# The first block's beginning rearranged in a two-branch kernel (state-space convolution plus a Mish feed-forward)

## The chip, the cores and the metric

The kernel runs on one core of one Trainium2 chip. The metric is the device time of one execution in microseconds. Its engines are PE (matrix products), DVE (VectorE), ACT (ScalarE), POOL (GpSimd) and SP (which here only issues transfers). ACT and POOL issue transfers too.

## What is computed

The input u has 2048 rows of 640 values. Each row is normalized; the result xn goes through two branches, whose sum is added to u.

```
xn  = (u - mean) / sqrt(var + 1e-5)                      # per row of 640
A   = causal convolution of xn over the rows, one kernel per column,
      K = 2 * Re(sum_n C_n * exp(A_n * dt * l)), plus xn * D_skip
h   = xn @ w1 + b1                                       # w1: 640 x 1728
B   = (h * tanh(softplus(h))) @ w2                       # w2: 1728 x 640
out = u + A + B
```

## The kernel before

**Tiles.** The 2048 rows are worked off in four blocks (or chunks) of TB = 512 columns of the transposed x, so that the 640 columns of x lie in KD = 5 groups ("channels") of 128 partitions. The 1728 hidden values lie in NF = 14 tiles f, of 128 or (f = 8) 64. A block multiplies w1's tile f with x (15 products of 512 columns; names h and tr in the trace), sends the result through a chain of activation steps on ACT and DVE, and multiplies it with w2 into five accumulators (acc). Single precision is reached by splitting each operand into a high and a low half-precision part: `hi_...` rounds on ACT, `lo_...` takes the rest on DVE, and each product is made three times: hh, lh (weight low), hl (x low). In blocks 1 to 3, pairs of tiles f go through a scheme with fewer products (the five parts `one` to `four` of `mm1_pair`), for which sums of weights and of x are prepared.

**Side work.** Beside this stand: the weight roundings in block 0; the statistics and normalization of the next chunk's x; the convolution, which for these inputs becomes two running sums per channel and chunk ("skip" steps: `skip_a` on ACT L709 to L711, the scans `skip_b` and `skip_c` on DVE at L715 and L719, `skip_e` at L729, `skip_d` on ACT); the 29 checks of the weights' size (`load_chk`, `chk` on ACT at L675 and L678) whose result decides at the end whether a general version must run; POOL's accumulating transfers that join the parts.

**Order.** The order of every engine is fixed when the kernel is built. For the beginning (block 0's products f = 0, 1, 2 and all before them) it is written out by hand, in the part that the change replaces. From there the class `Plan` sets it: each step has an engine, an assumed cost, the steps that it needs, buffers that it takes and drops, and a due time; whenever an engine is free in the plan's own clock, the ready step with the earliest need is put next. PE's order is given, and other steps get due times from it. `pl.end["m1", 0, f]` and the clocks in `Plan({...})` say when the handwritten part is assumed to end on each engine. `edge` and `t0, t1` give due times to the skip steps and the checks, as positions in PE's order (`start(b, f)` is the begin of block b's tile f).

**The beginning.** X0 holds block 0's four row tiles of 128 x 640. `stats0(i)` takes the statistics of tile i on DVE (L597 to L599, L1260) and the power -0.5 on POOL (L1261). `norm0(i)` normalizes on DVE (L1201). `norm0_a(i)`, which is defined but not called, does it on ACT. `to_t0(i)` transposes tile i on PE, five channels, into the accumulators' banks (L1217). `hi0(k, c)` and `lo0(k, c)` round channel k of one half: CA is columns 0 to 255 (tiles 0 and 1), CB columns 256 to 511 (tiles 2 and 3). `mm1_part(f, kinds, c, ks)` makes products (L755). `load_w1`, `hi_w1` (L522), `lo_w1` (L526) bring and split the weights. `fill(n)` keeps PE busy with products of the identity matrix. The queues of SP and ACT share the loads: column halves of tiles 0 and 1, then the row halves (64 partitions on each queue) of w1(0), tile 2, w1(1) and tile 3.

Of the kernel before, what the change touches and what calls it, by code (L numbers as in the profile page):

```python
# [422 lines left out]
def body(ctx: ExitStack, tc: tile.TileContext, x, xT, logA, Aim, Cr, Ci, logdt, vec, w1, w1T, w2, w2T, out):  # L423
# [65 lines left out]
    NCHK = NF + 3 * KD  # L489
    pl = Plan({"PE": 20.8, "ACT": 16.1, "DVE": 17.9, "SP": 15.0, "POOL": 15.0})  # L490
    tiles = lambda pool, name, n, shape: [pool.tile(shape, F32, name=f"{name}{j}") for j in range(n)]
# [421 lines left out]
    def whole():  # L913
# [53 lines left out]
        for f in range(3):  # L967
            pl.end["m1", 0, f] = (16.95, 18.55, 20.75)[f]

# [167 lines left out]
        for k in range(KD):  # L1137
            add(("x0s", k), V, 0.62, x0_sum, k, rel=start(0, 9))
        edge = [start(1, 4), start(2, 0), start(2, 11), start(3, 5), start(3, 11)]
        todo = [(c, k) for c in range(NB) for k in range(KD)]  # L1140
# [20 lines left out]

        t0, t1 = start(1, 4), start(3, 11)
        for j in range(NCHK):
# [33 lines left out]
    mv0 = tmp.tile([P, NT, 2], F32, name="mv0")  # L1197
    rs0 = tmp.tile([P, 2, NT], F32, name="rs0")

    def norm0(i):  # L1200
        v.tensor_scalar(X0[:, i], X0[:, i], mv0[:, i, 0:1], rs0[:, 0, i:i + 1], op0=OP.subtract, op1=OP.mult)  # L1201

    def norm0_a(i):
        v.scalar_tensor_tensor(rs0[:, 1, i:i + 1], mv0[:, i:i + 1, 0], -1.0, rs0[:, 0, i:i + 1], op0=OP.mult, op1=OP.mult)
        a.activation(X0[:, i], X0[:, i], AF.Identity, bias=rs0[:, 1, i:i + 1], scale=rs0[:, 0, i:i + 1])

# [18 lines left out]
    def load_x0(i):  # L1225
        for e, c in ((sp, slice(0, P // 2)), (a, slice(P // 2, P))):
            e.dma_start(X0[c, i], xr[0, i, c])

    def fill(n):
        for _ in range(n):  # L1230
            pe.matmul(TR[:, 0:P], ident, ident, start=True, stop=True)

    with tc.manual_schedule():

        for i in range(2):
            sp.dma_start(X0[:, i, 0:320], xr[0, i, :, 0:320])  # L1236
            a.dma_start(X0[:, i, 320:D], xr[0, i, :, 320:D])
        for f in range(6):
            pl.take("w", ("w1", f))
            if f < 2:  # L1240
                pl.take("w", ("w2", f))
        load_w1(0, (sp, a))
        load_x0(2)
        load_w1(1, (sp, a))
        load_x0(3)
        a.activation(warm, one, AF.Sigmoid)
        load_w1(2)
        sp.dma_start(cv[:, 0:24], vec)
        load_w1(3)
        load_w2(0)  # L1250
        load_w1(4)
        load_w2(1)
        load_w1(5)
        S = [list(stat_ops(mv0, X0[:, i], i)) for i in range(NT)]

        def stats0(i):
            for o in S[i]:
                o()
            r = rs0[:, 0, i:i + 1]
            v.tensor_scalar(r, mv0[:, i:i + 1, 1], EPS, None, op0=OP.add)  # L1260
            g.tensor_tensor(r, r, half, op=OP.pow)  # L1261

        fill(11)
        stats0(0)
        stats0(1)
        norm0(0)
        to_t0(0)
        hi_w1(0)
        norm0(1)
        to_t0(1)  # L1270
        for k in KS:
            hi0(k, CA)
        lo_w1(0)
        stats0(2)
        mm1_part(0, ("hh", "lh"), CA, start=True, ks=KS)
        hi_w1(1)
        lo0(KS[0], CA)
        lo0(KS[1], CA)
        mm1_part(1, ("hh",), CA, start=True)
        for f in range(2):  # L1280
            mm1_part(f, ("hl",), CA, ks=KS[:2])
        hi_w1(2)
        stats0(3)
        norm0(2)
        mm1_part(2, ("hh",), CA, start=True)
        to_t0(2)
        lo0(KS[2], CA)
        norm0(3)
        lo0(KS[3], CA)
        lo0(KS[4], CA)  # L1290
        mm1_part(2, ("hl",), CA, ks=KS[:2])
        for f in range(3):
            mm1_part(f, ("hl",), CA, ks=[KS[2]])
        to_t0(3)
        for k in KS[3:]:
            for f in range(3):
                mm1_part(f, ("hl",), CA, stop=f == 0 and k == KS[4], ks=[k])
        for k in KS:
            hi0(k, CB)
        lo_w1(1)  # L1300
        hi_w1(3)
        mm1_part(0, ("hh", "lh"), CB, start=True, ks=KS)
        for k in KS:
            lo0(k, CB)
        mm1_part(1, ("hh",), CB)
        mm1_part(0, ("hl",), CB, stop=True, ks=KS)
        lo_w1(2)
        lo_w1(3)
        for f in (1, 2):
            if f > 1:  # L1310
                mm1_part(f, ("hh",), CB)
            mm1_part(f, ("hl",), CB)
            mm1_part(f, ("lh",), slice(0, TB), stop=True)
# [39 lines left out]
```

## Time and profile before

| what | us |
|---|---|
| median of 3 runs | 359.85 (359.8 to 360.6) |
| the profiled execution | 359.29 |
| its span, first to last instruction | 357.5 |
| PE busy | 350.6 |
| DVE busy | 311.1 |
| ACT busy | 296.3 |
| POOL busy | 50.4 |

A row of the timeline gives the start and the length of one instruction or of several merged ones, its engine, line and operands, and in brackets how long the engine had been idle and what ended that. "PEld" is a weight load, which overlaps the products. "SPq" and "ACTq" are issues of transfers. Lengths of pipelined products overlap, so their distance, not their length, tells the cost. A row of the busy time in stretches gives the stretch, its length, each engine's busy time with its count of instructions, the granted clock of PE, the share of DMA time and GB/s. Line numbers are those of the kernel before.

### The profile page before, as it was taken

Reading aid. Unit: us, or ns where it says so; the run is one execution under the profiler, and the core shown is the slowest. Engines: PE = TensorE matmul, PEld = TensorE weight load, DVE = VectorE, ACT = ScalarE, POOL = GpSimd, SP = SyncE. Lnnn points to the kernel's source line nnn. Section 1 sums busy time; section 2 is a strip of 40 time slices with the busy share of each in tenths; the row PEclk is TensorE's granted clock in tenths of the full one; section 3 lists DMA queues with packets and bytes.
Section 4 is the critical chain, followed back from the end, with each engine's and each line's share of the span. In section 5 each row is a group of like instructions: output and inputs, shape, how many; then the busy total and the mean of one; then the engine's idle time right before and its main releaser. Section 6 shows DMA issues by size and latency. Waiting matters only on the chain.

```text
span 357.5 us, 6018 instructions
## 1 busy us (share of the span) xinstructions
PE 350.6 (98%) x2167; PEld 211.5 (59%) x2167; DVE 311.1 (87%) x585; ACT 296.3 (83%) x614; POOL 50.4 (14%) x72
## 2 busy tenths in 40 slices
PE   7999999999999999999999999999999999999995
PEld 6754444444666665665566666566566666566543
DVE  5989989989998999999999986899997888775552
ACT  3599999978488799889989897989978989868740
POOL 2100020000013041000103343000003552000000
PEclk9999999999999999999999999999999999999999
DMA  7879975105109954911256973941111994201003
GB/s 238 279 240 296 337 247 174 73 1 183 39 21 194 335 165 127 296 24 39 64 179 128 202 181 91 278 170 35 33 35 20 166 232 89 55 0 31 0 16 141
DMA packets 26036, 48.75 MB, mean 136 GB/s; under 512 B 3576, under 2 KB 6928, under 8 KB 26000
## 3 DMA queue, kind: packets, MB, share of 16 engines
q1 hardware_dynamic: 19152, 34.21, 29.8%
q0 software_dynamic: 6240, 13.11, 17.8%
q10 hardware_dynamic: 608, 0.98, 0.8%
q8 instruction: 19, 0.31, 0.4%
q14 instruction: 17, 0.14, 0.2%
HBM read 39.10 MB, written 5.26 MB: 124 GB/s over the span
## 4 chain that ended last, share of the span: by engine, by line
PE 95%; DMA 1%; DVE 1%; SPq 0%; ACT 0%; issue 0%; DVEq 0%
PE acc L825 48%; PE h L793 18%; PE h L773 14%; PE tr L793 12%; DMA x<-in_A_u_dram 1%; PE h L755 1%; PE tr L755 1%; PE acc L1217 0%; PE acc L839 0%; PE acc L836 0%; PE acc L837 0%; DVE w1l L526 0%; DVE st L598 0%; SPq L1236 0%; DVE st L597 0%
## 5 line engine op out<-in xcount | busy, mean ns | idle before, releaser
L825 PE MATMUL acc<-hi,w2h 128*128 128x512 f16 x273 | 100.9, 379 | 0.0
L825 PE MATMUL acc<-hi,w2l 128*128 128x512 f16 (+1 forms) x265 | 99.7, 379 | 0.0
L825 PE MATMUL acc<-lo,w2h 128*128 128x512 f16 x253 | 93.3, 379 | 0.0
L825 PEld LDWEIGHTS <-w2h 128*128 128x128 f16 x526 | 51.2, 98 | 48.4 <-issue 1.3
L863 ACT ACTIVATE s<-h,cv 128x512 f32<-128x512 f32 (+1 forms) x51 | 30.9, 605 | 23.6 <-PE h L793 18.4
L793 PEld LDWEIGHTS <-w1h 128*128 128x128 f16 x432 | 42.3, 98 | 10.7
L887 DVE SCALAR_TENSOR_TENSOR A<-p,A 128x512 f32<-128x512 f32 (+1 forms) x56 | 38.2, 682 | 7.2 <-ACT p L882 7.0
L825 PEld LDWEIGHTS <-w2l 128*128 128x128 f16 x273 | 25.6, 98 | 30.7 <-issue 1.1
L872 ACT ACTIVATE p<-s,kc 128x512 f32<-128x512 f32 (+1 forms) x56 | 40.1, 715 | 0.5
L882 ACT ACTIVATE p<-p,kc 128x512 f32<-128x512 f32 (+1 forms) x56 | 40.0, 714 | 0.2
L877 ACT ACTIVATE p<-p,kc 128x512 f32<-128x512 f32 (+1 forms) x56 | 39.9, 713 | 0.2
L905 DVE SCALAR_TENSOR_TENSOR lo<-A,hi 128x512 f16<-128x512 f32 x52 | 35.3, 680 | 3.6 <-ACT hi L894 3.3
L867 DVE SCALAR_TENSOR_TENSOR A<-h,bs,s 128x512 f32<-128x512 f32 (+1 forms) x51 | 33.0, 647 | 6.2 <-ACT s L863 6.0
L894 ACT ACTIVATE hi<-A 128x512 f16<-128x512 f32 (+1 forms) x56 | 34.9, 624 | 3.6 <-DVE A L887 3.4
L518 POOL DMA_DIRECT2D r<-in_xT_dram x15 | 13.7, 1094 | 126.8 <-ACT r L736 60.3
L773 PEld LDWEIGHTS <-w1h 128*128 128x128 f16 (+1 forms) x174 | 15.3, 99 | 20.3 <-issue 3.3
L715 DVE TENSOR_TENSOR_SCAN g<-g,car,kc 128x512 f32<-128x512 f32 x20 | 25.6, 1278 | 1.1 <-ACT g L709 1.1
L793 PEld LDWEIGHTS <-w1l 128*128 128x128 f16 x216 | 21.1, 98 | 8.4 <-issue 0.3
L719 DVE TENSOR_TENSOR_SCAN g<-g,car,g 128x512 f32<-128x512 f32 x20 | 25.5, 1276 | 0.1
L793 PE MATMUL tr<-xh,w1h 128*128 128x256 f16 x90 | 24.5, 273 | 0.1
L793 PE MATMUL tr<-xl,w1h 128*128 128x256 f16 x90 | 24.5, 273 | 0.0
L793 PE MATMUL tr<-xh,w1l 128*128 128x256 f16 x90 | 24.5, 273 | 0.0
(174 smaller groups left out, 728.7 us busy)
## 6 DMA issues: line engine op xcount, KB each, us to landing
w<-in_w_dram SPq DMA_DIRECT2D x23, 320.0 KB, 4.7
w<-in_w2T_dram SPq DMA_DIRECT2D x15, 288.0 KB, 6.4
w<-in_B_w_dram SPq DMA_DIRECT2D x13, 320.0 KB, 3.5
w<-in_w1T_dram SPq DMA_DIRECT2D x13, 320.0 KB, 6.6
x<-in_A_u_dram SPq DMA_DIRECT2D x12, 320.0 KB, 5.0
xt<-in_xT_dram SPq DMA_DIRECT2D x15, 256.0 KB, 5.5
r<-in_xT_dram POOLq DMA_DIRECT2D x15, 256.0 KB, 6.0
xt<-r POOLq DMA_DIRECT2D x15, 256.0 KB, 4.1
```

Of the source, the lines that this page charges most:

```text
L715: v.tensor_tensor_scan(g1[:, 1:], g1[:, 1:], zero.to_broadcast([P, TB]), car[:, 1, k:k + 1], op0=OP.add, op1=OP.add)
L773: pe.matmul(o, w, x, start=(j == 0), stop=(j == len(order) - 1))
L793: pe.matmul(o, p, q, start=start and n == 1, stop=n == 3 * len(w), skip_group_check=True)
L825: pe.matmul(o, w, x, start=start, stop=stop)
L863: a.activation(pl["s", b, f][:n, c], src(b, f) if h is None else h, AF.Sigmoid, bias=cv[:n, f:f + 1], scale=1 / SH)
L867: v.scalar_tensor_tensor(pl["A", b, f][:n, c], src(b, f) if h is None else h, bs[:n, f:f + 1], pl["s", b, f][:n, c], op0=OP.add, op1=OP.mult)
L872: a.activation(pl["p", b, f][:n], pl["s", b, f][:n], AF.Arctan, bias=one[:n], scale=-1.0)
L877: a.activation(p, p, AF.Square, bias=pi4[:n], scale=2.0)
L882: a.activation(p, p, AF.Tanh, bias=mb[:n], scale=MG)
L887: v.scalar_tensor_tensor(A, pl["p", b, f][:n], MC, A, op0=OP.add, op1=OP.mult)
L894: a.activation(hi[:n], A, AF.Copy, scale=MA * SA / SH)
L905: v.scalar_tensor_tensor(lo, A, MA * SA / SH, hi[:n], op0=OP.mult, op1=OP.subtract)
```

## The change

The two column halves of tile 0 are each split in two row halves, one on each queue; tile 1 keeps its column halves. Weights and tiles 2 and 3 come whole on SP's queue, in the order w1(0), w1(1), tile 2, tile 3. The warm-up activation (with the table load) follows directly on ACT's three issues. Tiles 0, 2 and 3 are normalized on ACT, whose `norm0_a` no longer uses DVE; tile 1 stays on DVE. `hi_w1(0)`, `hi_w1(1)` and `lo_w1(0)` stand ahead of the rounding of x, and for each channel the products hh and lh of f = 0 and hh of f = 1 follow its rounding. The low weight parts are spread between the low parts of x, and their products of half CA come earlier. The plan's clocks, the due times of the skip steps of chunks 1 to 3 and the beginning of the weight checks are changed.

```diff
-    pl = Plan({"PE": 20.8, "ACT": 16.1, "DVE": 17.9, "SP": 15.0, "POOL": 15.0})
+    pl = Plan({"PE": 19.95, "ACT": 15.3, "DVE": 16.8, "SP": 15.0, "POOL": 15.0})
...
-            pl.end["m1", 0, f] = (16.95, 18.55, 20.75)[f]
+            pl.end["m1", 0, f] = (17.0, 18.1, 19.9)[f]
...
-        edge = [start(1, 4), start(2, 0), start(2, 11), start(3, 5), start(3, 11)]
+        edge = [start(1, 4), start(2, 0), start(3, 2), start(3, 6), start(3, 13)]
...
-        t0, t1 = start(1, 4), start(3, 11)
+        t0, t1 = start(1, 0), start(3, 11)
...
+    nm0 = tmp.tile([P, 2, NT], F32, name="nm0")
...
     def norm0_a(i):
-        v.scalar_tensor_tensor(rs0[:, 1, i:i + 1], mv0[:, i:i + 1, 0], -1.0, rs0[:, 0, i:i + 1], op0=OP.mult, op1=OP.mult)
-        a.activation(X0[:, i], X0[:, i], AF.Identity, bias=rs0[:, 1, i:i + 1], scale=rs0[:, 0, i:i + 1])
+        a.activation(nm0[:, 0, i:i + 1], mv0[:, i:i + 1, 0], AF.Copy, scale=-1.0)
+        a.activation(nm0[:, 1, i:i + 1], nm0[:, 0, i:i + 1], AF.Identity, scale=rs0[:, 0, i:i + 1])
+        a.activation(X0[:, i], X0[:, i], AF.Identity, bias=nm0[:, 1, i:i + 1], scale=rs0[:, 0, i:i + 1])
...
     def load_x0(i):
-        for e, c in ((sp, slice(0, P // 2)), (a, slice(P // 2, P))):
-            e.dma_start(X0[c, i], xr[0, i, c])
+        sp.dma_start(X0[:, i], xr[0, i])
...
-        for i in range(2):
-            sp.dma_start(X0[:, i, 0:320], xr[0, i, :, 0:320])
-            a.dma_start(X0[:, i, 320:D], xr[0, i, :, 320:D])
+        for c in (slice(0, 320), slice(320, D)):
+            for e, p in ((sp, slice(0, P // 2)), (a, slice(P // 2, P))):
+                e.dma_start(X0[p, 0, c], xr[0, 0, p, c])
+        sp.dma_start(X0[:, 1, 0:320], xr[0, 1, :, 0:320])
+        a.dma_start(X0[:, 1, 320:D], xr[0, 1, :, 320:D])
...
-        load_w1(0, (sp, a))
+        a.activation(warm, one, AF.Sigmoid)
+        load_w1(0)
+        load_w1(1)
         load_x0(2)
-        load_w1(1, (sp, a))
         load_x0(3)
-        a.activation(warm, one, AF.Sigmoid)
...
-        def stats0(i):
-            for o in S[i]:
+        def stats0(i, done=0):
+            for o in S[i][done:]:
...
-        fill(11)
+        fill(10)
         stats0(0)
         stats0(1)
-        norm0(0)
+        norm0_a(0)
         to_t0(0)
-        hi_w1(0)
         norm0(1)
         to_t0(1)
+        hi_w1(0)
+        hi_w1(1)
+        lo_w1(0)
         for k in KS:
             hi0(k, CA)
-        lo_w1(0)
+            mm1_part(0, ("hh", "lh"), CA, start=k == KS[0], ks=[k])
+            mm1_part(1, ("hh",), CA, start=k == KS[0], ks=[k])
+        hi_w1(2)
+        mm1_part(2, ("hh",), CA, start=True)
         stats0(2)
-        mm1_part(0, ("hh", "lh"), CA, start=True, ks=KS)
-        hi_w1(1)
+        for o in S[3][:2]:
+            o()
         lo0(KS[0], CA)
...
+        stats0(3, 2)
+        norm0_a(2)
+        norm0_a(3)
+        hi_w1(3)
+        for k, w in zip(KS, (None, None, 1, 2, 3)):
+            if k != KS[0]:
+                lo0(k, CA)
             for f in range(3):
                 mm1_part(f, ("hl",), CA, stop=f == 0 and k == KS[4], ks=[k])
+            if k == KS[1]:
+                to_t0(2)
+            if w:
+                lo_w1(w)
+                if w < 3:
+                    mm1_part(w, ("lh",), CA)
+                if w == 1:
+                    to_t0(3)
         for k in KS:
             hi0(k, CB)
...
+            mm1_part(0, ("hh", "lh"), CB, start=k == KS[0], ks=[k])
+            mm1_part(1, ("hh",), CB, ks=[k])
         for k in KS:
             lo0(k, CB)
...
+        mm1_part(0, ("hl",), CB, stop=True)
+        mm1_part(1, ("lh", "hl"), CB, stop=True)
+        mm1_part(2, ("hh", "lh", "hl"), CB, stop=True)
         a.activation(bs, cv[:, 0:NF], AF.Copy, scale=SH)
...
-        pl.drop(("w1", f), 17.0)
+        pl.drop(("w1", f), 15.0)
```

More of the change, by code (lines that the diff above doesn't have):

```diff
@@ L1274, in body @@
+        mm1_part(2, ("hh",), CA, start=True)
         stats0(2)
-        mm1_part(0, ("hh", "lh"), CA, start=True, ks=KS)
-        hi_w1(1)
+        for o in S[3][:2]:
+            o()
         lo0(KS[0], CA)
[L1278 to L1295, printed above, removed]
+        stats0(3, 2)
[5 more added lines that the diff above has]
+                lo0(k, CA)
             for f in range(3):
                 mm1_part(f, ("hl",), CA, stop=f == 0 and k == KS[4], ks=[k])
+            if k == KS[1]:
[6 more added lines that the diff above has]
+                    to_t0(3)
@@ L1298, in body @@
         for k in KS:
             hi0(k, CB)
-        lo_w1(1)
-        hi_w1(3)
-        mm1_part(0, ("hh", "lh"), CB, start=True, ks=KS)
+            mm1_part(0, ("hh", "lh"), CB, start=k == KS[0], ks=[k])
+            mm1_part(1, ("hh",), CB, ks=[k])
         for k in KS:
             lo0(k, CB)
[L1305 to L1313, printed above, removed]
+        mm1_part(0, ("hl",), CB, stop=True)
```

## The prediction

> **What bounds the kernel now.** I read the page's busy times first, then the chain of waits, then the busy time in stretches, and last the timeline of the first 20 us, where the change acts.
>
> ```profile
> PE 350.6 (98%) x2167; PEld 211.5 (59%) x2167; DVE 311.1 (87%) x585; ACT 296.3 (83%) x614; POOL 50.4 (14%) x72
> ...
> 20.75 3.24 PE h L773 x15
> ...
> 96.23 1.97 PE h L793 x18
> ...
> 353.05 0.12 PE h L847
> ```
>
> ```profile
> 90.00:96.20 6.20, 6.20 (x42) 3.84 (x40) 5.99 (x16) 2.68 (x7) 0.00 (x0) 1.00 0.20 56
> 96.20:108.60 12.40, 12.40 (x87) 8.24 (x85) 12.08 (x44) 9.46 (x19) 2.61 (x3) 1.00 0.18 53
> ...
> 114.10:174.20 60.10, 60.04 (x391) 37.18 (x389) 58.77 (x103) 55.51 (x121) 9.10 (x13) 1.00 0.54 158
> 174.20:241.30 67.10, 67.10 (x450) 43.39 (x448) 61.27 (x101) 59.62 (x134) 14.79 (x19) 1.00 0.63 168
> 241.30:271.20 29.90, 29.90 (x195) 18.50 (x193) 28.66 (x47) 27.49 (x62) 0.00 (x0) 1.00 0.11 31
> 271.20:295.90 24.70, 24.70 (x170) 16.40 (x169) 20.66 (x31) 22.03 (x51) 12.85 (x16) 1.00 0.80 159
> 295.90:336.90 41.00, 41.00 (x277) 26.04 (x275) 28.68 (x55) 32.75 (x70) 3.28 (x5) 1.00 0.18 34
> ```
>
> PE is busy 98%, and in the stretches (length, then PE, weight loads, DVE, ACT, POOL, clock, DMA share, GB/s) its busy time equals the length, but for 0.06 us in the third row. So from 20.75, where the planned part begins with the products of f = 3, to 353.17, PE simply works off 332.4 us. Two things follow. The re-spread side work has nothing to win (0.06 us); it can only lose. And what the beginning wins is handed through to the end: every microsecond by which the products of f = 0..2 are done earlier than 20.75 is a microsecond of the span, as long as the planned part stays full.
>
> **The beginning, before.**
>
> ```profile
> 0.72 0.87 SPq L1236 DMA_DIRECT2D x<-in_A_u_dram  x2
> ...
> 3.70 0.49 DVE L597 BATCH_NORM_STATS2 st<-x 128x6 f32<-128x320 f32 x1 [2.73 <-DMA x<-in_A_u_dram]
> ...
> 4.94 0.48 DVE L597 BATCH_NORM_STATS2 st<-x 128x6 f32<-128x320 f32 x1
> 5.11 0.57 POOL L1261 TENSOR_TENSOR rs<-rs,kc 128x1 f32<-128x1 f32 x1 [3.61 <-DVE rs L1260]
> 5.21 1.28 ACT L1246 ACT_TABLE_LOAD   x1 [5.21 <-DMA x<-in_A_u_dram]
> ...
> 6.09 0.15 DVE L1260 TENSOR_SCALAR rs<-mv 128x1 f32<-128x1 f32 x1
> 6.16 0.60 DVE L1201 TENSOR_SCALAR x<-x,mv,rs 128x640 f32<-128x640 f32 x1
> 6.33 0.86 POOL L1261 TENSOR_TENSOR rs<-rs,kc 128x1 f32<-128x1 f32 x1 [0.65 <-DVE rs L1260]
> ...
> 6.62 0.72 ACT L522 ACTIVATE w1h<-w 128x640 f16<-128x640 f32 x1
> ...
> 7.23 0.61 DVE L1201 TENSOR_SCALAR x<-x,mv,rs 128x640 f32<-128x640 f32 x1 [0.46 <-POOL rs L1261]
> ...
> 7.75 0.82 DVE L526 SCALAR_TENSOR_TENSOR w1l<-w,w1h 128x640 f16<-128x640 f32 x1
> ...
> 7.89 0.76 PE L1217 MATMUL acc<-ident,x 128*128 128x128 f32 x5 [0.30 <-DVE x L1201]
> ...
> 8.26 1.49 ACT L1220 ACTIVATE xh<-acc 128x256 f16<-128x256 f32 x5 [0.92 <-PE acc L1217]
> ...
> 8.49 0.49 DVE L597 BATCH_NORM_STATS2 st<-x 128x6 f32<-128x320 f32 x1
> ...
> 8.70 0.27 PE L755 MATMUL h<-xh,w1h 128*128 128x256 f16 x1
> ...
> 9.60 0.77 ACT L522 ACTIVATE w1h<-w 128x640 f16<-128x640 f32 x1
> ...
> 9.72 0.74 DVE L1223 SCALAR_TENSOR_TENSOR xl<-acc,xh 128x256 f16<-128x256 f32 x2
> ...
> 10.42 0.72 PE L755 MATMUL h<-xh,w1h 128*128 128x256 f16 x5 [0.24 <-ACT w1h L522]
> ...
> 14.57 1.74 DVE L1223 SCALAR_TENSOR_TENSOR xl<-acc,xh 128x256 f16<-128x256 f32 x5
> ...
> 16.23 1.54 DVE L526 SCALAR_TENSOR_TENSOR w1l<-w,w1h 128x640 f16<-128x640 f32 x2
> ```
>
> The first product stands at 8.70. From there PE owes 90 products of 256 columns (30 for each f, a 512-column one counted twice) at 1.97 / 18 = 0.109, which is 9.8, and the ten transposes of tiles 2 and 3, 1.1 (next fence): 10.9 us. It takes 20.75 - 8.70 = 12.05, so 1.15 us is lost to waits and to products paced by x's rounding (1.49 for five). That loss and the 8.70 are what the change can alter.
>
> ```profile
> 13.58 0.55 PE acc L1217 x5
> ...
> DMA to landing us min/median/max: 3.1/3.1/3.1
> ...
> DMA to landing us min/median/max: 3.1/4.4/5.3
> ...
> 2.50:3.90 1.40, 1.40 (x8) 1.40 (x8) 0.20 (x1) 0.00 (x0) 0.00 (x0) 1.00 1.04 374
> 4.30:6.40 2.10, 2.10 (x11) 1.91 (x9) 1.96 (x8) 1.19 (x1) 0.64 (x2) 1.00 0.95 326
> ...
> L724 ACT COPY car<-g 128x1 f32<-128x1 f32 x20 | 3.8, 190 | 1.1 <-DVE g L719 1.1
> ...
> 174.20:241.30 67.10, 7.67 (x6) 1.00 0.63 168
> ...
> 271.20:295.90 24.70, 3.84 (x3) 1.00 0.80 159
> ...
> 322.39 0.73 DVE L729 SCALAR_TENSOR_TENSOR xt<-xt,cc,g 128x512 f32<-128x512 f32 x1
> ```
>
> **The change, part by part.**
>
> *Tile 0 in four pieces.* Its first columns are now the first transfer of both queues: 160 KB before statistics can start instead of 320 KB, at 374 GB/s 0.44 us earlier than 3.70 at best. Against that, tile 1 is each queue's third issue instead of its second, one issue (0.87 / 2 = 0.44) later; at 3.1 us to landing (first landing row, the column halves of tiles 0 and 1) it comes at about 4.75, and DVE wants it at 4.94. So the chain through tile 1, which matters, starts between 0.2 earlier and, if the 64-row pieces are slow, 0.15 later (320 KB at 326, the stretch in which 64-row halves moved, instead of 374). I take 0.15 earlier: on a queue with bytes waiting, landing goes rather by bytes than by issue.
>
> By the Trainium skill (SBUF — State Buffer, "Can I just issue two DMAs to hit both halves?") two transfers on partitions 0 to 63 and 64 to 127 serialize, only 6% faster than one at 196 GB/s; by that, 208 GB/s, tile 0 would take an estimated 0.7 us longer and the sum would be 359.6. The 326 GB/s of the second stretch speak against it.
>
> *norm0 of tile 0 goes from DVE to ACT.* The second POOL power took 0.86 beside the 0.60 of DVE's normalization, the first 0.57 with none beside it. With tile 0 on ACT, I take 0.57: tile 1 normalizes 0.29 earlier, at 6.94, and its transposes start at 7.60. ACT does tile 0 after the first power (5.68): two one-column steps (0.19, of which the first needs no power and hides before it) and 640 columns at the 0.72 of L522, done at 6.6; PE's transposes of tile 0 at 6.7 stand before 7.60, so this is hidden. The table load goes ahead of all this, since ACT now issues three transfers and not eight. Fewer filler matmuls cost nothing: PE waits for tile 0 anyway.
>
> An Identity is nowhere in this trace; it is bounded by L522's 0.72 below and by two more table loads of 1.28 above. By the Trainium skill (ScalarE: Activation LUTs, "Table sets: the hidden batching unit") identity and copy are in every set, so that no load would be added; no run here shows it yet.
>
> *Two weight roundings ahead of x's.* ACT does hi_w1(0) and hi_w1(1) at 0.65 each (back to back) from 6.5: free at 7.8. x's first channel is ready 0.37 after the transposes begin (8.26 - 7.89), at 7.97. Queued behind hi_w1(1) are the five roundings of x, and behind them all products; it must land by 7.15. w1(1) is the fourth tile in order of bytes (1.3 MB at 374 GB/s, 3.5 us; tile 0's 320 KB take 0.9 of the 3.70 at which they are there, so the first byte and the landing together account for 2.8: it lands at 6.3), where before it shared the queues with tile 2. lo_w1(0) on DVE ends at 8.35. First product: 8.26 - 0.29 + 0.44 = 8.41, less 0.15 for the load: 8.26.
>
> *Products follow x's rounding.* Three products (0.33) now follow each rounding (0.27 to 0.30), so PE is the slower of the two and stays full: 15 products end at 9.9, where before 10 ended at 10.18, and the 0.24 wait for w1h(1) goes. What is late next is hi_w1(2), on ACT behind the roundings (ends 9.9): a gap of 0.1. Then lo0 on DVE: between 8.1 and its first step stand tile 2's statistics (1.23, from 8.49 to 9.72 before) and two of tile 3's (0.8), so the first low part ends at 10.5 and the second, behind 0.4 of statistics, at 11.3: gaps of 0.1 and 0.4. From there weight lows (0.73) and x lows (0.37) alternate on DVE ahead of PE, and tiles 2 and 3 are normalized by ACT (0.95 each) beside the products. DVE loses three normalizations (1.8 us) and ends its last low parts of x near 16.4 with no weight work behind; before it ended at 17.77. PE then is the bound: 8.26 + 10.9 + 0.6 of gaps = 19.76 against 20.75, a gain of **1.0 us**, between 0.6 (8.41 and 0.9 of gaps) and 1.4.
>
> *Plan.* Its clocks are moved earlier by 0.8 to 1.1 us, as the preamble is; weight tiles come free earlier too, so the loads that waited for them go earlier. The 29 weight checks (ACT 0.9 each with their load of 320 KB) start at block 1's first product instead of its fifth: some three of them land between 89 and 114, where ACT was busy 2.68 of 6.20 and 9.46 of 12.40 and DMA a fifth. Nothing is paid there; without that cover each would take 0.9 from the activation chain. The skip work of chunks 1 to 3 is moved later; see the third rival.
>
> *Sum.* Profiled execution: 359.29 with a span of 357.5. 359.29 - 1.0 = 358.3; the median of the runs shown stands 0.56 higher, 359.85 - 1.0 = **358.9**.
>
> **Rivals.**
>
> *The beginning wins more.* If landing goes by bytes alone (0.44) and DVE's second low part comes without the 0.4 gap, PE starts the planned part at 19.3: 358.4. For it: DVE has 1.8 us less. Against: tile 1's later issue. Chance 0.16.
>
> *The loads eat the gain.* If w1(1) takes the 5.3 us of the slowest w1 load from its issue near 2.9, it lands at 8.2 instead of 7.15, and all of x's rounding waits 1.05: 360.0, chance 0.04. An extra table load for Identity, 1.28, would end near there too, chance 0.01. Were the two 64-row halves of tile 0 to move one behind the other, at half of 374, its 320 KB would take 0.86 longer: 359.8, chance 0.02; the SBUF page of the Trainium skill stands for this case. Against: the 5.3 us were spent behind other bytes in a full queue, and halves moved 326 GB/s. Together 0.07.
>
> *The side work starves PE: slower.* Place: block 3, 271.2 to 295.9, into which the new edges put the due times of all five skip steps of chunk 2. One costs DVE 1.28 + 1.28 + 0.74 = 3.3 us. Before, three lay there (3.84 is three scans), with DVE at 20.66. Five make 20.66 + 6.6 = 27.3 in 24.7 us: 2.6 too much, ACT's 22.03 likewise near full, and mish steps that release PE come late: 358.9 + 2.6 = 361.5. It decides if steps really wait for their due times; then more than 2.0 us of it must show on PE to be slower by 0.3%. Against: steps run early when DVE is free (six were done between 174 and 241 before), and DVE has 12 us free after 296. Chance 0.19.
>
> **How the numbers follow.** Forecast 0.58, its own range 358.5 to 359.3. A difference of 0.3%, 1.08 us, is about what a measurement of this kernel can tell from no change; that edge, 358.77, lies inside the forecast's range, a little on its faster side: 0.26 faster, 0.32 same. The first rival gives 0.16 faster; the second 0.06 same and 0.01 slower; the third 0.17 slower and 0.02 same. Together faster 0.42, same 0.40, slower 0.18. The range runs from the first rival's 358.2 to 361.0, inside the third, which leaves out some 0.17.
>
> **What would show it.** Right: second power near 0.57; first product near 8.3; 15 products without a gap; f = 3 beginning at 19.5 to 20.0; PE busy time equal to the length in every later stretch. Wrong: ACT idle before hi_w1(1) on a transfer; a table load beside the Identity; PE idle, or the chain of waits leaving PE, between 270 and 300.

## The result, and the profile after

The changed kernel takes 361.31 us (median; 360.89 to 362.56) against 359.82 in the same comparison (359.42 to 360.6): a ratio of 1.0044, with a 95% interval of 1.0035 to 1.0053. It is **slower**, by 1.5 us (0.44%, above the 0.3% that the prediction took as its edge), where 0.9 us less was forecast; the time lies 0.3 above the range. The profiled execution took 361.25, its span is 359.5, so it stands for its median better than that of before (359.29) does.

The page: PE's busy time and the beginning of the chain of waits.

```profile
PE 351.1 (98%) x2175; PEld 213.1 (59%) x2175; DVE 308.5 (86%) x582; ACT 301.3 (84%) x623; POOL 50.5 (14%) x72
...
3.09 5.05 DMA w<-in_w_dram
9.22 3.19 PE h L755 x15
```

The busy time in stretches, three of the plan that the third rival and its surroundings are about (columns as before: stretch, length, PE, weight loads, DVE, ACT, POOL, clock, DMA share, GB/s):

```profile
174.20:241.30 67.10, 67.10 (x449) 43.35 (x448) 61.53 (x102) 59.10 (x131) 14.77 (x19) 1.00 0.60 163
271.20:295.90 24.70, 24.70 (x170) 16.40 (x168) 20.63 (x31) 21.56 (x49) 10.98 (x14) 1.00 0.68 129
295.90:336.90 41.00, 41.00 (x277) 26.04 (x276) 31.95 (x58) 34.23 (x77) 4.90 (x6) 1.00 0.21 46
```

PE is full in each, and between 271.2 and 295.9 DVE works 20.63 us, not the third rival's 27.3. So that rival's mechanism did not occur, and most of the loss is in the beginning. The timeline of it, with the rows that answer to those of before and ACT's new steps (`norm0_a` is now L1205 to L1207, the transposes L1219, x's rounding L1222):

```profile
0.72 1.21 SPq L1238 DMA_DIRECT2D x<-in_A_u_dram  x2
3.40 0.49 DVE L597 BATCH_NORM_STATS2 st<-x 128x6 f32<-128x320 f32 x1 [2.43 <-DMA x<-in_A_u_dram]
4.52 0.49 DVE L598 BATCH_NORM_STATS2 st<-x 128x6 f32<-128x320 f32 x1 [0.63 <-DMA x<-in_A_u_dram]
5.36 0.48 DVE L597 BATCH_NORM_STATS2 st<-x 128x6 f32<-128x320 f32 x1
...
6.13 0.29 ACT L1206 ACTIVATE nm<-nm,rs 128x1 f32<-128x1 f32 x1 [0.64 <-POOL rs L1264]
6.46 0.92 ACT L1207 ACTIVATE x<-x,nm,rs 128x640 f32<-128x640 f32 x1
6.75 0.56 POOL L1264 TENSOR_TENSOR rs<-rs,kc 128x1 f32<-128x1 f32 x1 [0.65 <-DVE rs L1263]
7.29 0.72 ACT L522 ACTIVATE w1h<-w 128x640 f16<-128x640 f32 x1
7.43 1.35 PE L1219 MATMUL acc<-ident,x 128*128 128x128 f32 x10 [1.35 <-ACT x L1207]
8.16 0.74 ACT L522 ACTIVATE w1h<-w 128x640 f16<-128x640 f32 x1 [0.15 <-DMA w<-in_w_dram]
8.81 1.46 ACT L1222 ACTIVATE xh<-acc 128x256 f16<-128x256 f32 x5
9.22 0.27 PE L755 MATMUL h<-xh,w1h 128*128 128x256 f16 x1 [0.44 <-ACT xh L1222]
...
19.28 0.69 ACT L863 ACTIVATE s<-h,cv 128x512 f32<-128x512 f32 x1 [2.24 <-PE h L755]
...
21.80 1.24 PE L773 MATMUL h<-xh,w1h 128*128 128x512 f16 x5
25.43 0.38 PE L825 MATMUL acc<-hi,w2h 128*128 128x512 f16 x1 [0.23 <-ACT hi L894]
```

Tile 0's second columns come late (DVE waits 0.63), ACT needs 1.2 for tile 0, the second weight tile keeps ACT waiting, and the first product is at 9.22 instead of 8.70. Then 15 products take 3.19 (the chain of waits), though each needs 0.109. Stretches of the beginning show why:

```profile
2.50:3.90 1.40, 1.40 (x8) 1.40 (x8) 0.49 (x1) 1.01 (x1) 0.00 (x0) 1.00 0.85 223
...
9.00:10.00 1.00, 0.78 (x5) 0.63 (x5) 0.97 (x3) 1.00 (x5) 0.00 (x0) 0.71 1.04 378
10.00:11.00 1.00, 1.00 (x7) 0.69 (x6) 0.96 (x5) 0.76 (x2) 0.55 (x1) 0.50 1.03 405
...
12.00:13.00 1.00, 1.00 (x7) 0.74 (x6) 1.00 (x3) 0.91 (x3) 0.32 (x1) 0.58 1.03 410
```

The granted clock (third number from the right) is 0.50; from the shares 0.71 and 0.58 at the ends it was halved from about 9.42 to 12.84. And in 2.5 to 3.9 the loads move 223 GB/s where they moved 374.

The planned part begins at 21.80 instead of 20.59. From f = 3's first row to the start of DVE's last step it is 332.77 (before 332.60), so the profiles differ by 1.21 in the beginning, 0.17 behind it, and 0.62 in the tail from the start of DVE's last step (4.93 against 4.31).

### The profile page after: what moved, and what is told of

It reads as the page before. It is cut to its first block, busy times and chain, and to the rows that moved or that the text cites. A ratio compares the mean times of both kernels' runs of the same rounds, so it can differ in the third digit from the quotient of the medians.

```text
span 359.5 us, 6053 instructions
## 1 busy us (share of the span) xinstructions
PE 351.1 (98%) x2175; PEld 213.1 (59%) x2175; DVE 308.5 (86%) x582; ACT 301.3 (84%) x623; POOL 50.5 (14%) x72
## 4 chain that ended last, share of the span: by engine, by line
PE 94%; ACT 2%; DMA 1%; SPq 1%; DVE 0%; issue 0%
PE acc L825 48%; PE h L793 18%; PE h L773 13%; PE tr L793 11%; PE h L755 2%; DMA w<-in_w_dram 1%; PE tr L755 1%; ACT w1h L522 0%; ACT s L863 0%; ACT w2h L529 0%; ACT p L872 0%; SPq L1238 0%; PE acc L1219 0%; PE acc L839 0%; PE acc L837 0%; PE acc L836 0%
## 5 line engine op out<-in xcount | busy, mean ns | idle before, releaser
L825 PE MATMUL acc<-hi,w2h 128*128 128x512 f16 x273 | 100.9, 379 | 0.2 <-ACT hi L894 0.2
L825 PE MATMUL acc<-hi,w2l 128*128 128x512 f16 (+1 forms) x265 | 99.7, 379 | 0.0
L825 PE MATMUL acc<-lo,w2h 128*128 128x512 f16 x253 | 93.3, 379 | 0.0
L825 PEld LDWEIGHTS <-w2h 128*128 128x128 f16 x526 | 51.2, 98 | 48.4 <-issue 1.3
L793 PEld LDWEIGHTS <-w1h 128*128 128x128 f16 x432 | 42.3, 98 | 10.7
L825 PEld LDWEIGHTS <-w2l 128*128 128x128 f16 x273 | 25.6, 98 | 31.1 <-issue 1.6
L793 PEld LDWEIGHTS <-w1l 128*128 128x128 f16 x216 | 21.1, 98 | 8.2
L793 PE MATMUL tr<-xh,w1l 128*128 128x256 f16 x90 | 24.5, 273 | 0.0
L793 PE MATMUL tr<-xl,w1h 128*128 128x256 f16 x90 | 24.5, 273 | 0.0
L793 PE MATMUL tr<-xh,w1h 128*128 128x256 f16 x90 | 24.5, 273 | 0.0
```

What stands on the lines that cost most here:

```text
L793: pe.matmul(o, p, q, start=start and n == 1, stop=n == 3 * len(w), skip_group_check=True)
L825: pe.matmul(o, w, x, start=start, stop=stop)
```

## The experiments

The times are medians, each beside the kernel before in the same comparison (359.66 to 359.92). "f = 3" is the begin of the planned part and "rest" the time from there to the start of DVE's last step, both from the profile. A beginning differs by some tenths between executions, with the landing of its loads; single profiles show mechanisms, the medians what they cost. Where an expectation speaks of 6 filling products, read 10 (so e16_load_fill7 has fewer, not more).

| kernel | us | ratio, 95% interval | first product | f = 3 | rest |
|---|---|---|---|---|---|
| before | 359.82 | | 8.70 | 20.59 | 332.60 |
| the change | 361.31 | 1.0035 to 1.0053 | 9.22 | 21.80 | 332.77 |
| e1_fill13 | 360.64 | 1.0012 to 1.0035 | 9.54 | 21.25 | 332.77 |
| e2_load | 360.28 | 1.0002 to 1.0024 | 8.90 | 20.60 | 332.77 |
| e3_dvenorm | 361.36 | 1.0023 to 1.0057 | 9.96 | 22.23 | 332.77 |
| e4_respread | 361.79 | 1.0034 to 1.0060 | 8.99 | 21.54 | 334.18 |
| e5_fill8 | 359.83 | 0.9991 to 1.0009 | 8.94 | 20.78 | 332.60 |
| e6_old_dues | 363.04 | 1.0075 to 1.0113 | 9.41 | 21.12 | 334.72 |
| e7_load_old_dues | 362.09 | 1.0049 to 1.0077 | 8.53 | 20.26 | 334.70 |
| e8_edges | 361.47 | 1.0029 to 1.0056 | 8.50 | 20.40 | 334.48 |
| e9_checks | 360.93 | 1.0015 to 1.0035 | 8.49 | 20.39 | 333.80 |
| e10_w1_later | 360.14 | 1.0000 to 1.0019 | 8.26 | 20.19 | 332.77 |
| e11_f0_first | 359.56 | 0.9986 to 1.0004 | 8.43 | 20.36 | 332.38 |
| e12_hold | 364.67 | 1.0126 to 1.0155 | 9.02 | 24.65 | 332.77 |
| e13_f0_dve | 359.70 | 0.9989 to 1.0007 | 8.55 | 20.65 | 332.38 |
| e14_f0_fill13 | 359.54 | 0.9985 to 1.0004 | 8.44 | 20.79 | 332.38 |
| e15_halves | 361.14 | 1.0026 to 1.0059 | 10.06 | 22.81 | 332.99 |
| e16_load_fill7 | 360.43 | 1.0011 to 1.0035 | 9.20 | 21.78 | 332.77 |
| e17_halves_fill13 | 360.70 | 1.0016 to 1.0034 | 8.96 | 20.94 | 332.38 |

### The change with one part put back

**e1_fill13**: more products of the identity narrow PE's gap ahead of the transposes (0.82 instead of 1.35 in the profiles).

```diff
-        fill(10)
+        fill(13)
```

> The changed kernel with 13 filler matmuls in place of 10, so that PE has work until about 7.5 instead of 6.09 (each filler took 0.46 us) and does not idle 1.3 us ahead of the transposes. Theory B (half clock): the granted clock, 0.50 from 9.4 to 12.8 in the changed kernel, stays at 1.00; its first 15 products take 1.6 to 1.7 instead of 3.19, and if the products are what the beginning waits for, the products of f = 3 begin 1.0 to 1.5 earlier than 21.80 and the time falls to about 360.0. Theory A (late start: loads and the normalization on ACT): the clock is restored but DVE and ACT set the pace from there, f = 3 begins at most 0.5 earlier, the time stays above 360.7.

**e2_load**: tile 0 comes in column halves of 128 rows again, all else as changed.

```diff
-        for c in (slice(0, 320), slice(320, D)):
-            for e, p in ((sp, slice(0, P // 2)), (a, slice(P // 2, P))):
-                e.dma_start(X0[p, 0, c], xr[0, 0, p, c])
-        sp.dma_start(X0[:, 1, 0:320], xr[0, 1, :, 0:320])
-        a.dma_start(X0[:, 1, 320:D], xr[0, 1, :, 320:D])
+        for i in range(2):
+            sp.dma_start(X0[:, i, 0:320], xr[0, i, :, 0:320])
+            a.dma_start(X0[:, i, 320:D], xr[0, i, :, 320:D])
```

> The changed kernel with tile 0 loaded as before, in two column halves of all 128 rows, one per queue (w1 and tiles 2 and 3 still whole on SP). Theory A with the row halves as its cause: the second statistics step starts at 4.1 instead of 4.52, everything up to the first product comes 0.4 to 0.5 earlier (8.75 instead of 9.22), w1(1) lands before 7.9 instead of 8.14, and the time falls by 0.4 to 0.6 (360.8). If the transfers were limited by bytes alone, nothing moves: within 0.2 of 361.3. Theory B alone expects a gain only if the granted clock is back at 1.00.

**e3_dvenorm**: `norm0(0)` on DVE in place of `norm0_a(0)`.

> The changed kernel with tile 0 normalized on DVE, as before (tiles 2 and 3 stay on ACT). Theory A with ACT's normalization as its cause: ACT loses 0.29 + 0.92 ahead of the weight roundings, tile 0's transposes start near 7.2 instead of 7.43; but the second power is again beside a DVE normalization (0.86 instead of 0.56), and the rounding of w1(1) still waits for its transfer (8.14), so the first product moves by less than 0.2 and the time by less than 0.3 (361.0 to 361.6). If ACT's normalization was the main loss, 0.6 or more (360.7 or less).

With 13 fillers 0.67 us go (f = 3 is 0.55 earlier in the profile, at full rate; the time lies between the two cases of the expectation), with the column halves 1.03, with tile 0 on DVE nothing (361.36). The timeline of e2_load shows what the column halves bring:

```profile
3.62 0.49 DVE L597 BATCH_NORM_STATS2 st<-x 128x6 f32<-128x320 f32 x1 [2.65 <-DMA x<-in_A_u_dram]
4.03 0.47 DVE L598 BATCH_NORM_STATS2 st<-x 128x6 f32<-128x320 f32 x1
...
6.93 1.35 PE L1219 MATMUL acc<-ident,x 128*128 128x128 f32 x10 [1.62 <-ACT x L1207]
7.84 0.74 ACT L522 ACTIVATE w1h<-w 128x640 f16<-128x640 f32 x1 [0.33 <-DMA w<-in_w_dram]
8.90 0.27 PE L755 MATMUL h<-xh,w1h 128*128 128x256 f16 x1 [0.62 <-ACT xh L1222]
...
10.42 0.27 PE L755 MATMUL h<-xh,w1h 128*128 128x256 f16 x1
```

DVE no longer waits inside tile 0, the transposes come 0.5 earlier, and the 15 products start within 1.52, at full rate. But the second weight tile still keeps ACT, now 0.33. The profile of e3_dvenorm has the half clock as the change has it, so it tells only that DVE's normalizing doesn't cure it.

### The side work's due times

**e4_respread** is the kernel before with the change's `edge` and `t0`; **e8_edges** has `edge` alone, **e9_checks** `t0` alone. **e6_old_dues** is the change with both of before, **e7_load_old_dues** is e2_load with both of before.

```diff
-        edge = [start(1, 4), start(2, 0), start(2, 11), start(3, 5), start(3, 11)]
+        edge = [start(1, 4), start(2, 0), start(3, 2), start(3, 6), start(3, 13)]
...
-        t0, t1 = start(1, 4), start(3, 11)
+        t0, t1 = start(1, 0), start(3, 11)
```

> The kernel before with only the due times changed: the edges of the skip steps and the begin of the weight checks as in the change. The prediction's third rival (five skip steps of chunk 2 between 271 and 296 starve PE): 1 to 2.6 slower than before, 360.8 to 362.4, PE idle in that stretch. What the trace of the changed kernel says (PE full in every stretch from 30 on): within 0.3 of 359.8.

> The kernel before with only the edges of the skip steps changed. With edges and checks together it was 2.1 slower: PE waited 1.53 for the check's product (L700) behind scans on DVE, and the tail grew by 0.6. If the edges are the cause (later skip steps crowd the check's last steps on DVE, and their transfers reach into the tail): 361.2 to 362.0. If the earlier checks are: 359.7.

> The kernel before with only the begin of the weight checks changed, from block 1's fifth product to its first. If the edges are the cause of the 2.1: within 0.3 of 359.7. If the checks are (their last one ended 316.6 to 317.2 instead of 313.99): 360.8 or more, with PE waiting at L700.

> The changed kernel with the due times of before (edges of the skip steps and begin of the checks); beginning and clocks as in the change. Theory C (the due times cost 0.6 in the tail, which after the last DVE step measured 4.5 against 3.9 us, whatever the beginning): 0.5 to 0.8 less than the changed kernel, about 360.7. Theory A/B alone (all of the loss lies in the beginning, the longer tail is chance): within 0.3 of 361.3.

> The changed kernel with tile 0 loaded as before and the due times of before. With the load alone it measured 360.28, products of f = 3 from 20.60 (before: 20.59), a wait of 0.23 for the activation of f = 0 and a tail of 4.6. Theory C: the tail returns to 3.9 and the time to 359.6 to 359.8, level with before. If the due times do nothing here: 360.3. A gain over before of 0.5 or more would need PE to begin f = 3 earlier than 20.1, which neither theory expects.

Each new pair is slower, e6 and e7 against their expectations: on the old beginning the new due times cost 1.7 together (1.5 for `edge` alone, 0.9 for `t0` alone, by the ratios), on the new beginning the old ones cost 1.7 (and 1.8 on e2_load). The rest shows it too, 1.2 to 1.95 longer than with the pair that belongs together. Each timeline has one place where PE waits for more than 1 us: those of e4_respread, e6_old_dues and e8_edges, in this order (e9_checks waits 1.15 at L700, e7_load_old_dues 1.40):

```profile
324.42 0.38 PE L700 MATMUL tr<-ok,ones 128*128 128x1 f32 x2 [1.53 <-DVE ok L697]
```

```profile
324.54 0.38 PE L700 MATMUL tr<-ok,ones 128*128 128x1 f32 x2 [1.41 <-DVE ok L697]
```

```profile
300.25 0.27 PE L793 MATMUL tr<-xh,w1h 128*128 128x256 f16 x1 [1.27 <-ACT h L1030]
```

L700 is the product that joins the weight checks. PE's order fixes its place, and DVE does the check's one-column steps late. In e4_respread two scans and the step L729 lie between two of them (DVE's timeline):

```profile
319.93 0.16 DVE L694 SCALAR_TENSOR_TENSOR c<-q 128x4 f32<-128x4 f32 x1
320.01 1.28 DVE L715 TENSOR_TENSOR_SCAN g<-g,car,kc 128x512 f32<-128x512 f32 x1
321.39 1.28 DVE L719 TENSOR_TENSOR_SCAN g<-g,car,g 128x512 f32<-128x512 f32 x1
322.71 0.75 DVE L729 SCALAR_TENSOR_TENSOR xt<-xt,cc,g 128x512 f32<-128x512 f32 x1
323.38 0.29 DVE L694 SCALAR_TENSOR_TENSOR c<-q 128x4 f32<-128x4 f32 x3
```

The same two places in the timelines of before, and then of the change:

```profile
319.59 0.16 DVE L697 TENSOR_TENSOR ok<-ok,z 128x1 f32<-128x1 f32 x1
322.00 0.28 PE L700 MATMUL tr<-ok,ones 128*128 128x1 f32 x2
```

```profile
322.94 0.15 DVE L697 TENSOR_TENSOR ok<-ok,z 128x1 f32<-128x1 f32 x1
323.38 0.28 PE L700 MATMUL tr<-ok,ones 128*128 128x1 f32 x2
```

So the new due times aren't at fault: they fit the new beginning, but with 0.44 from one start to the other where there were 2.41.

### The rest of the beginning

**e5_fill8**: the kernel before with 8 fillers instead of 11, to bring about the gap alone.

> The kernel before with 8 filler matmuls in place of 11: PE has no work from about 5.2 to 6.8 instead of from 6.51. Everything else, the order of every engine included, is as before. Theory B (idle time of PE ahead of the products lets the granted clock fall): in some runs the clock falls to 0.5 for some 3.4 us as in the changed kernel (9.4 to 12.8), the mean clock of these runs is 0.995 or less where the kernel before has 0.996 to 1.000, and the median is 0.3 to 1.0 above 359.8. If the idle time has nothing to do with the clock: clocks as before and the time within 0.3 of 359.8.

No change in the time, though its profile has half rate: the ten transposes take 2.40 and three products follow at 0.21 (timeline).

```profile
6.75 2.40 PE L1217 MATMUL acc<-ident,x 128*128 128x128 f32 x10 [1.51 <-DVE x L1201]
8.94 0.42 PE L755 MATMUL h<-xh,w1h 128*128 128x256 f16 x1
9.15 0.42 PE L755 MATMUL h<-xh,w1l 128*128 128x256 f16 x1
```

The f = 3 products come 0.19 later. In this execution half rate cost little: it covered the transposes and few products, and x's rounding is what the products wait for.

**e10_w1_later**: e2_load with `hi_w1(1)`, and hh of f = 1, behind the rounding of x. **e11_f0_first**: the same for half CB, so that f = 0's products end before f = 1's.

```diff
-        hi_w1(1)
         lo_w1(0)
         for k in KS:
             hi0(k, CA)
             mm1_part(0, ("hh", "lh"), CA, start=k == KS[0], ks=[k])
-            mm1_part(1, ("hh",), CA, start=k == KS[0], ks=[k])
+        hi_w1(1)
+        mm1_part(1, ("hh",), CA, start=True)
...
             mm1_part(0, ("hh", "lh"), CB, start=k == KS[0], ks=[k])
-            mm1_part(1, ("hh",), CB, ks=[k])
...
-        mm1_part(1, ("lh", "hl"), CB, stop=True)
+        mm1_part(1, ("hh", "lh", "hl"), CB, stop=True)
```

> The changed kernel with tile 0 loaded as before, and with the rounding of w1(1) behind the rounding of x instead of ahead of it (the products hh of f = 1 follow it then, as before). In the run with the load alone the first rounding of x stood at 8.48 behind w1(1), which waited for its transfer until 7.84, and the first product at 8.90. If the weight rounding ahead of x is what holds the products: rounding of x from 7.6, first product near 8.2 (lo_w1(0) ends at 8.36, so 8.4 for the second), f = 3 from 20.0 to 20.3, time 359.7 to 360.0. If DVE's steps pace the beginning from there on: f = 3 at 20.5, time within 0.2 of 360.28.

> The kernel of the run before this one (tile 0 loaded as before, w1(1) rounded after x), and in the second half of the columns f = 0's products are ended before those of f = 1 begin. f = 0 then ends 0.5 earlier, its activation chain starts 0.5 earlier, and the wait of 0.23 for the activation of f = 0 at the first acc product, seen at 23.9 to 25.9 in every run of the new beginning, goes. Theory: 0.2 to 0.3 less than the run before this one, 359.5 to 359.7, level with the kernel before or just under it. If the wait is only handed on: no difference.

Without the wait for the second weight tile the first product comes 0.64 earlier in the profile, but the time hardly moves (360.28 to 360.14). With f = 0 ended first it falls to 359.56: the wait of 0.23 at the first L825, seen in the change at 25.43, is gone, and the rest is 0.39 shorter. The intervals of neighbouring kernels overlap, so the 0.58 is known to a few tenths only.

**e12_hold**: e2_load with a small transfer on SP's queue that waits for tile 0's statistics, ahead of tile 2's load.

> The changed kernel with tile 0 loaded as before, and with a small transfer on SP's queue that waits for the statistics of tile 0, so that tiles 2 and 3 and all later weights are issued at about 5.0 instead of 3.0. The prediction took w1(1) to land in order of bytes (6.3); it landed at 7.5 to 8.14. If transfers in flight share the engines, so that later ones delay earlier ones: w1(1) lands by 7.0, x's rounding starts near 7.6 instead of 8.48, but tile 2 comes later (DVE waits at 8.7 already) and the time may stay within 0.4 of 360.28. If they go in order of issue: w1(1) still lands at 7.5 to 7.8.

ACT rounds both weight tiles without a wait. The second one, issued at 2.11, landed at 7.13, against 7.81 in e2_load. But with the same loads and nothing held back it landed at 7.17 in e10_w1_later and at 7.05 in e11_f0_first, so it isn't shown that the hold brought it earlier: the landing differs that much between executions. The loads of the second weight tile in e12_hold and e11_f0_first (the last number is the time from issue to landing):

```profile
w<-in_w_dram SPq DMA_DIRECT2D x1, 320.0 KB, 5.0
```

```profile
w<-in_w_dram SPq DMA_DIRECT2D x1, 320.0 KB, 4.9
```

The price of the hold is an empty queue afterwards (87 and 41 GB/s in 6 to 8 and 8 to 10), f = 3 at 24.65, and 4.4 us more than e2_load, far outside the 0.4 that was expected.

### What the row halves cost, and how

Five kernels on e11_f0_first and e2_load: **e13_f0_dve** (e11, tile 0 normalized on DVE), **e14_f0_fill13** (e11, 13 fillers), **e15_halves** (e11, tile 0 in row halves), **e16_load_fill7** (e2_load, 7 fillers), and **e17_halves_fill13** (e15, 13 fillers). Their edits are lines that stand above.

> The best version so far (tile 0 in column halves, hi_w1(1) behind x's rounding, the products of f = 0 ended ahead of those of f = 1 where the chunks of x's rounding run), with tile 0 normalized on VectorE again. If the engine that normalizes tile 0 matters once the loads are right: tile 1 waits for tile 0's 0.57 on VectorE, and the second power again takes 0.86, so the transposes come 0.3 to 0.6 later or, with ScalarE's 0.92 gone, at the same time: 359.2 to 360.1. If it doesn't, as when it was tried in the changed kernel itself (361.36 against 361.31): 359.6 within 0.3.

> The same best version with 13 filling products instead of 6. If TensorE's gap ahead of the transposes still costs a stretch of half clock in some executions: 0.2 to 0.6 less than 359.56, so 359.0 to 359.4. If the beginning is paced by x's rounding, so that a slower TensorE is hidden: 359.56 within 0.2.

> The best version with tile 0 in halves of 64 rows, as in the changed kernel: its loads alone put back. If the 1.03 that the column halves brought is their landing alone (0.36, the difference to the changed kernel with 13 filling products): 359.9. If it is landing and half clock together: 360.4 to 360.6, with a granted clock near 0.5 in the first products.

> The change with tile 0 in column halves, and 7 filling products instead of 6, so that TensorE's gap lies elsewhere against the gate's window. If half clock at the first products costs 0.67 wherever it falls: 360.28, or about 360.9 where its profile shows the clock near 0.5 there. If it is the landing that counted: 360.28 within 0.2, whatever the clock column shows.

> The best version with tile 0 in halves of 64 rows (361.14, where 359.56 stands with column halves), and 13 filling products instead of 10. If the 1.58 is landing (1.0, by the transposes' start in the two profiles, 7.88 against 6.87) and half clock behind the longer gap (the rest): 360.5, with the first products at 0.11 from one another. If the late landing is all of it: 361.1. If it is all half clock: 359.6 to 359.8.

The row halves cost 1.58 here (361.14 against 359.56). With 13 fillers on both sides they cost 1.16 (360.70 against 359.54); no profile with 13 fillers has half rate behind the fillers, so this is taken for the late landing. The other 0.42 goes with the fillers, and by the profiles it is half rate, but the intervals of e15 and e17 overlap, so the split is argued and not measured clear of noise. Both times are above what was expected of e15 (360.6 at most) and e17 (360.5). The profile of e17 is of its fastest execution (359.91). Rows of e15_halves, then of e17_halves_fill13:

```profile
1.46 4.64 PE L1232 MATMUL tr<-ident 128*128 128x128 f32 x20 [1.46 <-POOL ident masks.py:199]
4.96 0.49 DVE L598 BATCH_NORM_STATS2 st<-x 128x6 f32<-128x320 f32 x1 [1.10 <-DMA x<-in_A_u_dram]
7.88 2.39 PE L1219 MATMUL acc<-ident,x 128*128 128x128 f32 x10 [1.78 <-ACT x L1207]
2.50:3.90 1.40, 1.40 (x8) 1.40 (x8) 0.49 (x1) 1.02 (x1) 0.00 (x0) 1.00 0.82 210
```

```profile
4.46 0.49 DVE L598 BATCH_NORM_STATS2 st<-x 128x6 f32<-128x320 f32 x1 [0.64 <-DMA x<-in_A_u_dram]
7.37 1.56 PE L1219 MATMUL acc<-ident,x 128*128 128x128 f32 x10 [0.20 <-ACT x L1207]
```

The fillers don't speed up the loads (210 and, in e17, 214 GB/s; 348 in e11_f0_first in the same stretch), only the rate of what follows. Once the loads are right, fillers gain nothing (e14 359.54) and neither does ACT or DVE for tile 0 (e13 359.70).

e16_load_fill7's twelve executions fall in two groups, seven from 359.88 to 360.48 and five from 361.27 to 361.81. Its profile is of the second, with the transposes at half rate, as are the products behind them (0.21 apart):

```profile
7.01 2.39 PE L1219 MATMUL acc<-ident,x 128*128 128x128 f32 x10 [2.21 <-ACT x L1207]
```

So with fewer fillers the half rate becomes a matter of the execution, at 1.2 us (f = 3 against e2_load's) to 1.45 (the groups' medians) in the new beginning. No profile is of the first group, and three of its seven executions list a mean clock of 0.992 or 0.993, which suggests a stretch at half rate in them too, at little cost.

What decides can be read from the traces. In every profile the fillers begin at half rate: their rows (two for each filler) lie 0.21 apart, as the 20 of e15_halves above, where the later ones of e2_load lie 0.11 apart. The trace's record of the granted clock starts with the first full clock, and the column counts the time before it as 1.00. This first full clock comes at 6.01 in the change, but at 9.69 in e5_fill8, 10.48 in e12_hold, 12.59 in e16_load_fill7 and 13.80 in e15_halves. In these four the transposes did not fall to half rate behind their gap; they had not left it yet. In the change and in e3_dvenorm the clock had been full and fell.

Each fall on record in the beginnings (the change, e3_dvenorm, e12_hold) lasts 3.41, so the beginnings can be cut into stretches of 3.41, counted from the first full clock. In the first 20 us of all 19 profiles, full rate follows a stretch at half rate in which PE was busy for 81% or more, and half rate goes on behind 78% or less; full rate goes on behind a stretch at full rate with 53% or more, and half rate follows 48% or less. Such stretches of the change, e2_load, e15_halves and e11_f0_first (behind the length stands PE's busy time):

```profile
6.01:9.42 3.41, 1.62 (x13) 1.31 (x13) 2.49 (x7) 3.10 (x7) 0.65 (x2) 1.00 1.01 360
```

```profile
4.33:7.74 3.41, 1.79 (x16) 1.54 (x15) 2.51 (x9) 2.05 (x4) 1.14 (x2) 1.00 0.95 316
```

```profile
6.97:10.39 3.42, 2.52 (x12) 2.39 (x13) 2.62 (x6) 2.38 (x5) 0.56 (x1) 1.00 1.00 361
```

```profile
3.21:6.62 3.41, 2.88 (x14) 2.58 (x13) 2.50 (x8) 1.22 (x3) 0.84 (x2) 1.00 0.98 325
```

Half rate follows the first (48%) and goes on behind the third (74%); full rate goes on behind the second (53%) and follows the fourth (84%). So the length of the gap alone doesn't decide, but how much PE works in the stretch that the gap falls into; and where the stretches lie differs from execution to execution (the first full clock comes at 4.33 in e2_load and at 6.62 in e11_f0_first, with the same loads and fillers).

## Why the prediction was wrong

**Bound: right, and used too far.** PE is full from f = 3 on, and what the beginning loses arrives at the end: e1 to e3 differ by f = 3 alone, with the same rest. "The re-spread side work has nothing to win" failed: the plan is laid anew when the beginning moves, and the old due times on the new beginning cost 1.7.

**Tile 0 in four pieces: the step that failed first.** Forecast 0.15 earlier, at worst 0.15 later. The first columns did come earlier (3.40 against 3.70), but the second 64-row pieces at 4.52, and tile 1's statistics began 0.42 later. The 326 GB/s that I held against serializing came from halves of 64 rows by all 640 columns, the 374 from 128 rows by 320 columns; pieces that have both 64 rows and 320 columns were in no row, and moved 210 to 224. The second rival priced serializing (0.86 later) with a chance of 0.02. By the Trainium skill (SBUF — State Buffer, "Can I just issue two DMAs to hit both halves?") two such transfers serialize; the trace agrees for these pieces, with 223 GB/s beside the 208 that the prediction worked out from it, but not for the whole-row halves of before (326). What sets the two apart wasn't tried. What the landing alone costs is known roughly: 0.36 in the change (e1 against e2, which has only ten fillers and may hold executions at half rate), 1.16 in the repaired beginning (e17 against e14).

**w1(1) in order of bytes: failed.** Forecast 6.3, needed by 7.15, landed 8.14 (3.09 + 5.05). That is the second rival's landing, but not its price of 1.05: ACT, late itself, waited 0.15 for it. By 8.14 about 1.7 MB had been moved (217 GB/s), where 1.3 MB had been issued up to and with w1(1), so loads issued later had moved beside it, and the order of bytes gave a landing 1.8 too early. With the column halves it landed between 7.05 and 7.95 in seven profiles, with the row halves between 8.04 and 8.46 in five; that it would land earlier with nothing behind it is not shown (e12_hold).

**The ScalarE normalization: mis-sized.** 0.19 + 0.72 was forecast, 0.20 + 0.29 + 0.92 measured, and tile 0 is done at 7.38, not at 6.6. By the Trainium skill (ScalarE: Activation LUTs, "What ACT_TABLE_LOAD costs") an immediate scale and bias take 186 ns and 0.833 ns an element, each one-column operand 93 ns more: for 640 columns and two, an estimated 0.905. The trace agrees with 0.92; L522, with none, was the wrong row. It cost nothing in the sum (e3, e13): tile 1, ready at 7.96 (7.35 + 0.61), is transposed right behind tile 0. The table load beside the Identity didn't occur, and the second power was 0.56 as forecast.

**The clock: not considered.** "Fewer filler matmuls cost nothing" left out that PE's work ahead of the products sets the rate behind it. In the change PE worked only 1.62 of the 3.41 us before 9.42, and the clock was half for the next 3.42, under 13 of the first 15 products. With 13 fillers it stayed full, and the median was 0.67 lower. In e15 against e17 the difference is 0.44, within their intervals. In e5 the full rate came at 9.69, after three products, so little was left to lose. By the Trainium skill (TensorE: Matmul & The Clock Gate, "What's actually happening") the clock is halved or full by windows of 3413 ns that run free; the length agrees (9.42 to 12.84), and so do the different places of the first full clock.

**10.9 plus 0.6: too little.** From the first product to f = 3 it takes 11.70 in e2_load and 11.93 in e11_f0_first, both without half rate, so the gaps are 0.8 to 1.0. In e10_w1_later the first product stands at 8.26, just as forecast, and f = 3 still begins at 20.19, not 19.76. The 20.75 that the gain was counted from is a row of the chain of waits, too; in the timeline f = 3 begins at 20.59 before, so 19.76 would have been a gain of 0.83, not 1.0.

**What the prediction did not list.** f = 0 now ended late, its sigmoid at 19.28 where the plan's clock has f = 0's products end at 17.0, so that ACT's chain held the first L825; and the check's product L700 is where PE waited in four of the five kernels with the other due times (e8 at L793).

The account: the change stands 1.75 above e11_f0_first, of which 1.03 is tile 0's load with its half rate, 0.14 the place of `hi_w1(1)` and 0.58 the order of f = 0 and f = 1. These are differences of medians from three comparisons, in which the kernel before itself differs by up to 0.26: the 0.14 is not clear of noise, and the others are known to a few tenths. e11_f0_first beats the change; with the kernel before it is level (0.9986 to 1.0004). Open stays the tail, 4.3 to 5.4 us in the profiles with no edit in it.

## What to carry to other kernels

Split a first load by columns and keep all 128 partitions in each transfer; take a rate only from pieces with the same rows and columns. Give a transfer's landing from its own rows, of several executions, not from the order of issue. Before PE is given less to do ahead of the first products, count how much of each stretch of 3.4 us it works; the length of one gap doesn't tell. When a handwritten beginning moves, take the plan behind it as new: look for the product with the least to spare, and compare each set of due times with the beginning that it was made for.

## What the runs showed of the hardware

- Two issues of 64 rows by 320 columns took 1.21, of 128 rows 0.87, and the loads then moved 210 to 224 GB/s (six profiles) against 347 to 386 (thirteen) in 2.5 to 3.9 us.
- PE begins at half rate in every profile. In stretches of 3.41 us, counted from the first full clock, full rate came behind 81% or more of PE's time busy and not behind 78% or less; it was lost behind 48% or less and kept behind 53% or more (first 20 us, 19 profiles). Shares between these were not seen there.
- The granted-clock column says 1.00 before the first full clock, also where ten transposes take 2.39 to 2.40 instead of 1.35 (e5_fill8, e12_hold, e15_halves, e16_load_fill7). The distance between like products shows the rate there.
- The same load of 320 KB, issued at 2.11 or 2.12 behind the same loads, landed anywhere from 7.05 to 7.95 (seven profiles).
- The two POOL powers ran 0.57 and 0.56 where DVE takes statistics or nothing beside them, and the second 0.86 again in e13_f0_dve and e3_dvenorm, where DVE normalizes beside it.
